# A linear-attention and SwiGLU block on one core: smaller first pieces, a split last block, and a scheduler that may wait

## The chip, the cores and the metric

The kernel runs on one core of a Trainium2 chip. The metric is the device time of one execution in microseconds (us). A profile's "span" is about 1.7 us shorter than that time. The profile of a kernel is one execution; the quoted times of the kernels before and after are of others.

## The reference

Layernorm of `x` (2048 x 1024), then two branches on the normalised `xn`: linear attention with 32 heads of 32, and a gated MLP with 3584 hidden columns. The output is `x + s * silu(mlp)`.

```python
def reference(A_x, A_wqkv, A_wo, B_x, B_w_gate, B_w_up, B_w_down):
    # ... qkv = xn @ wqkv; pq, pk = phi(q), phi(k); kv = pk^T v; s = (pq kv / pq z) @ wo
    # ... mlp = (silu(xn @ w_gate) * (xn @ w_up)) @ w_down
    x = A_x
    xn = _layernorm(x, axis=-1)
    s = _A_ref(xn, A_wqkv, A_wo)
    g = _silu(_B_ref(xn, B_w_gate, B_w_up, B_w_down))
    return x + s * g
```

## The kernel before

The matrix products are done with seven block products instead of eight (names `R00`, `T1` and so on). The sums and differences of blocks that this needs ("combinations") are VectorE's work, and PSUM results are joined by VectorE adds and ScalarE copies. The program runs in this order: a start (four x tiles: load, LN, transpose on TensorE, first k and v projections); the rest of k and v; then two passes over halves of the tokens, each with q, gate and up blocks, an `s` block (the attention output) and the down blocks.

Nothing is ordered by hand. Each operation is recorded with its reads and writes; a list scheduler that knows modelled durations fixes the order on every engine, and each engine then runs its list strictly in order. So a changed cost or position anywhere can reorder operations elsewhere.

```python
    def schedule(self):
        # ... dl: latest start for the modelled TensorE time; ready: when the inputs are there
            for e in self.ENGS:
                # ... TensorE has its own rule
                else:
                    rdy = [o for o in a if o.ready <= t]
                    o = min(rdy, key=lambda o: (o.dl - o.boost, o.idx)) if rdy else min(a, key=lambda o: (o.ready, o.dl))
```

```python
        def combos(v):          # four subtractions of whole 128x2048 blocks
            tt([v["R11"][1], v["R01"][1]], [v["T3"][1]], v["T3"][0], v["R11"][0], v["R01"][0], ALU.subtract, True)
            # ... T1, T2, T4

        # loads at the start, in this order
        for n, (fn, args) in enumerate(((x_load, (0,)), (x_load, (1,)), (wkv_load, (0, 1, 0)), (wkv_load, (0, 1, 1)),
                                        (wkv_load, (0, 0, 0)), (wkv_load, (0, 0, 1)), (x_load, (2,)), # ...

        # the normalisation of pq in pass p, hung on steps of the gate and up blocks
                if (k, n) == ("u", 1):
                    at = {"2_1": [partial(recip, p)]}
                if n == 2:
                    at = {w: [partial(normalise_part, p, "gu".index(k), h)] for h, w in enumerate(("2_1", "7_1"))}
                if (k, n) == ("g", 3):
                    at = {"2_1": [partial(combos, QV)], "7_1": [partial(x_inner, QV, qin, QIN_AT)]}
```

At the very end the last down product (step `4_1`) ends, ScalarE takes its silu, VectorE multiplies by `s`, TensorE transposes, VectorE adds `x`, and a store writes the result.

## Time and profile before

The time was 727.04 us in three runs (726.39 to 727.07).

| part of the profile | value |
|---|---|
| TensorE (PE) busy | 707.0 us, 97% of the span |
| VectorE (DVE) busy | 633.8 us, 87% |
| ScalarE (ACT) busy | 402.7 us, 56% |
| span | 725.4 us |

These lines are from the page of the kernel before: its span, the busy times, and the chain that ended last by engine.

```profile
span 725.4 us, 11190 instructions
PE 707.0 (97%) x4096; PEld 387.4 (53%) x4110; DVE 633.8 (87%) x1501; ACT 402.7 (56%) x773; POOL 14.2 (2%) x35
PE 87%; DVE 8%; DMA 2%; ACT 1%; issue 1%; SPq 0%; DVEq 0%
```

TensorE is the bound. Only its waits, the time before its first work and the time after its last are to be won. The Trainium skill (Trainium Kernel Development and Optimization, Performance Expectations) calls matmul busy time a bad metric for how close a kernel is to its roofline, because matmuls are pipelined. A 128x512 matmul is recorded as 0.379 us long but the next one starts 0.216 us later, so a wait of 0.16 us can hide inside "busy". I therefore also measured waits as the start of one matmul less the start of the one before, less the pace.

This is the table of waits, for TensorE alone, of the kernel before: waiting line, releaser, us in total, times, longest.

```profile
PE ps L233 <- DVE ps L376: 3.6, 6, 1.0
PE ps L233 <- ACT ps L365: 1.8, 2, 0.9
PE ps L233 <- ACT X L365: 1.6, 2, 1.2
...
PE ps L233 <- DMA H<-in_A_wqkv_dram: 0.4, 1, 0.4
```

Next come rows of the timeline of the kernel before, at its start: start in us, length, engine, line and operation; in brackets the idle time before it and what ended it.

```profile
3.58 0.69 DVE L680 BATCH_NORM_STATS2 stats<-W 128x6 f32<-128x512 bf16 x1 [2.39 <-DMA W<-in_A_x_dram]
...
6.43 0.55 DVE L694 TENSOR_SCALAR W<-W,mv,rstd 128x1024 f16<-128x1024 bf16 x1
...
8.12 2.76 PE L233 MATMUL ps<-H,X 128*128 128x512 bf16 x12 [0.47 <-ACT X L365]
8.25 1.23 DVE L376 TENSOR_TENSOR H<-H 128x2048 f16<-128x2048 bf16 x1 [0.97 <-DMA H<-in_A_wqkv_dram]
...
9.39 0.54 DVE L694 TENSOR_SCALAR W<-W,mv,rstd 128x1024 f16<-128x1024 bf16 x1
...
13.91 5.35 PE L233 MATMUL ps<-H,X 128*128 128x512 bf16 x23 [1.16 <-ACT X L365]
```

The LN of tile 1 (9.39) stands behind a 1.23 us combination, and TensorE later waits for that tile (13.91). The next rows, also of the timeline before, are those ahead of the `s` block of pass 1. Pass 2 repeats them near 534 us.

```profile
230.46 3.19 ACT L365 ACTIVATE H<-H,zc 128x512 bf16<-128x512 bf16 x5
...
234.47 0.64 ACT L365 ACTIVATE ps<-ps 128x512 f32<-128x512 f32 x1
...
235.16 1.90 PE L233 MATMUL ps<-X,W 128*128 128x512 f16 x8 [0.90 <-ACT ps L365]
...
235.74 1.22 DVE L376 TENSOR_TENSOR H<-H 128x2048 f16<-128x2048 f16 x1
...
236.87 0.69 DVE L376 TENSOR_TENSOR ps<-ps,TM 128x512 f32<-128x512 f32 x1
...
237.62 1.04 PE L233 MATMUL ps<-X,W 128*128 128x512 f16 x4 [0.56 <-DVE ps L376]
```

ScalarE works off five scale operations of the normalisation (3.19 us), and the copy that TensorE needs comes at 234.47. A whole combination on VectorE at 235.74 likewise delays the add at 236.87; the next wait ends at 237.62. The tail of the kernel before, in the same view:

```profile
718.31 0.60 ACT L365 ACTIVATE TM<-ps 128x512 f16<-128x512 f32 x1 [2.42 <-PE ps L233]
718.93 0.43 DVE L376 TENSOR_TENSOR TM<-TM 128x512 f16<-128x512 f16 x1 [2.26 <-ACT TM L365]
...
719.42 0.40 PE L240 MATMUL ps<-ident,TM 128*128 128x128 f16 x4 [1.15 <-DVE TM L376]
719.85 0.42 DVE L376 TENSOR_TENSOR TM<-ps,TM 128x512 bf16<-128x512 f16 x1 [0.49 <-PE ps L240]
```

### The profile page before, as it was taken

To read this page: it belongs to the slowest core of one execution; us is meant where nothing else is said; L and a number is where in the kernel's file an instruction comes from. 1 tells how busy PE (TensorE), PEld (TensorE's weight loads), DVE (VectorE), ACT (ScalarE), POOL (GpSimd) and SP (SyncE) were. 2 spreads that over 40 slices of the span, in tenths; PEclk is the share of its full clock that TensorE was granted. 3 is DMA by queue.
4 is the path that set the end of the run, shared out by engine and by line. 5 is a ranking of instruction groups with operands and counts; after the bars stand their busy time and mean duration, and the time that the engine had idled before them with its cause. 6 is when DMAs were issued, how large, how long until landed. Compare 5 with 4: busy or idle time off the path is not lost.

```text
span 725.4 us, 11190 instructions
## 1 busy us (share of the span) xinstructions
PE 707.0 (97%) x4096; PEld 387.4 (53%) x4110; DVE 633.8 (87%) x1501; ACT 402.7 (56%) x773; POOL 14.2 (2%) x35
## 2 busy tenths in 40 slices
PE   7999999999999999999999999999999999999996
PEld 3544445555555555556555454555555555565642
DVE  6999968989999998988966999999999989797852
ACT  3777554887659666654212156766786656531211
POOL 3101000000000000000000000000000000000000
PEclk9999999999999999999999999999999999999998
DMA  9345235145456343326595954231915241747563
GB/s 306 100 88 106 41 116 174 59 135 200 147 159 166 100 139 123 105 67 177 141 187 161 270 149 140 59 117 61 234 59 175 87 145 61 196 114 180 129 150 94
DMA packets 139127, 98.25 MB, mean 135 GB/s; under 512 B 33344, under 2 KB 136000, under 8 KB 139072
## 3 DMA queue, kind: packets, MB, share of 16 engines
q1 hardware_dynamic: 139072, 97.54, 47.9%
q8 instruction: 32, 0.52, 0.3%
q14 instruction: 23, 0.19, 0.1%
HBM read 77.59 MB, written 12.71 MB: 124 GB/s over the span
## 4 chain that ended last, share of the span: by engine, by line
PE 87%; DVE 8%; DMA 2%; ACT 1%; issue 1%; SPq 0%; DVEq 0%
PE ps L233 87%; DVE W L376 2%; DVE H L376 2%; DVE X L376 1%; DMA P<-x_scratch 1%; DMA H<-in_A_wqkv_dram 1%; DVE ps L376 1%; DVE TM L376 1%; SPq L379 0%; DVE P L376 0%; ACT TM L365 0%; ACT H L365 0%; PE ps L240 0%; ACT L365 0%; ACT ps L365 0%
## 5 line engine op out<-in xcount | busy, mean ns | idle before, releaser
L233 PE MATMUL ps<-X,W 128*128 128x512 f16 (+1 forms) x1344 | 289.9, 354 | 3.2 <-DVE ps L376 2.3
L365 ACT ACTIVATE TM<-ps 128x512 f16<-128x512 f32 (+2 forms) x353 | 186.1, 549 | 105.2 <-PE ps L233 103.1
L233 PE MATMUL ps<-H,W 128*128 128x512 f16 (+2 forms) x1090 | 218.4, 351 | 0.7 <-DVE ps L376 0.4
L376 DVE TENSOR_TENSOR W<-W 128x1024 f16<-128x1024 bf16 (+5 forms) x416 | 184.9, 479 | 5.5 <-PE ps L233 4.9
L233 PEld LDWEIGHTS ps<-X,W 128*128 128x128 f16 (+1 forms) x1344 | 130.4, 98 | 108.6 <-DVE ps L376 4.6
L233 PEld LDWEIGHTS ps<-H,W 128*128 128x128 f16 (+1 forms) x1096 | 106.6, 98 | 95.6 <-DVE ps L376 1.4
L365 ACT ACTIVATE ps<-ps 128x512 f32<-128x512 f32 (+1 forms) x172 | 84.7, 492 | 104.8 <-PE ps L233 101.3
L376 DVE TENSOR_TENSOR ps<-ps,TM 128x256 f32<-128x256 f32 (+1 forms) x250 | 130.7, 525 | 13.8 <-PE ps L233 12.5
L233 PE MATMUL ps<-P,W 128*128 128x256 f16 (+1 forms) x516 | 99.8, 319 | 1.2 <-ACT ps L365 0.9
L365 ACT ACTIVATE H<-ps 128x512 f16<-128x512 f32 (+1 forms) x126 | 75.0, 604 | 45.6 <-PE ps L233 45.5
L376 DVE TENSOR_TENSOR H<-H 128x1024 f16<-128x1024 f16 (+6 forms) x110 | 68.9, 640 | 1.1 <-DMA H<-in_A_wqkv_dram 1.0
L365 ACT ACTIVATE TM<-TM 128x512 f16<-128x512 f32 (+1 forms) x61 | 38.0, 629 | 52.6 <-DVE TM L376 52.6
L233 PEld LDWEIGHTS ps<-P,W 128*128 128x128 f16 (+1 forms) x516 | 50.0, 98 | 31.3 <-ACT ps L365 1.6
L233 PE MATMUL ps<-W 128*128 128x256 f16 (+1 forms) x330 | 62.1, 282 | 1.1 <-DVE ps L376 1.0
L376 DVE TENSOR_TENSOR H<-H,TM 128x512 f16<-128x512 f16 x112 | 45.1, 416 | 15.1 <-ACT H L365 14.9
L376 DVE TENSOR_TENSOR TM<-ps,TM 128x512 f32<-128x512 f32 (+1 forms) x60 | 40.7, 678 | 15.6 <-PE ps L233 15.1
L233 PEld LDWEIGHTS ps<-W 128*128 128x128 f16 (+1 forms) x330 | 31.5, 98 | 33.8 <-DVE ps L376 1.9
L233 PE MATMUL ps<-H,X 128*128 128x512 bf16 (+1 forms) x147 | 35.2, 379 | 2.2 <-ACT X L365 1.6
L233 PE MATMUL ps<-H,P 128*128 128x512 bf16 (+1 forms) x108 | 26.4, 379 | 0.1
L376 DVE TENSOR_TENSOR H<-ps,TM 128x512 f16<-128x512 f32 (+1 forms) x35 | 23.8, 680 | 2.2 <-PE ps L233 2.0
L233 PEld LDWEIGHTS ps<-H,X 128*128 128x128 f16 (+1 forms) x150 | 14.2, 98 | 18.5 <-ACT X L365 2.0
L376 DVE TENSOR_TENSOR TM<-TM,W 128x512 f16<-128x512 f16 (+1 forms) x39 | 14.1, 362 | 11.5 <-ACT TM L365 11.4
(95 smaller groups left out, 426.6 us busy)
## 6 DMA issues: line engine op xcount, KB each, us to landing
W<-in_B_w_gate_dram SPq DMA_DIRECT2D x14, 1024.0 KB, 5.3
W<-in_B_w_up_dram SPq DMA_DIRECT2D x13, 1024.0 KB, 5.6
W<-in_B_w_down_dram SPq DMA_DIRECT2D x14, 896.0 KB, 6.3
W<-in_A_x_dram SPq DMA_DIRECT2D x16, 256.0 KB, 3.0
H<-in_A_wqkv_dram SPq DMA_DIRECT2D x8, 512.0 KB, 8.0
H<-r_scratch SPq DMA_DIRECT2D x32, 128.0 KB, 3.8
W<-m_scratch SPq DMA_DIRECT2D x4, 1024.0 KB, 6.0
s_scratch<-TM SPq DMA_DIRECT2D x32, 128.0 KB, 2.6
```

The source lines that it names most:

```text
L233: last = h.matmul(o, l, r, start=st, stop=sp, skip_group_check=True)
L365: q = PL.op("act", reads, writes, lambda h: h.activation(o, i, func, **kw), nel(o) / (1000.0 if "bias" in kw or not isinstance(kw.get("sca ...
L376: return dve(reads, writes, lambda h: h.tensor_tensor(o, a, b, op), nel(o), 1.92 if fast else 0.96)
```

## The change

There are four parts. **Start:** x0 comes in two half loads on two queues; the first weight block is loaded ahead of x1; LN, transposes and first products work on smaller pieces. **Middle:** the normalisation and the combinations of the query blocks are issued earlier; combinations are cut in halves. **Tail:** the last down block finishes in two token halves, so the silu, the product, the transpose and the store after it are half as large. **Scheduler:** an engine other than TensorE and SP may leave a ready operation undone when a much more urgent one will be ready before it would end ("holding").

```diff
-TABLE, DMA_SLACK = 1.28, 2.0
+TABLE, DMA_SLACK, HOLD, YIELD = 1.28, 2.0, 0.1, 10
@@ schedule
-                    o = min(rdy, key=lambda o: (o.dl - o.boost, o.idx)) if rdy else min(a, key=lambda o: (o.ready, o.dl))
+                    soon = [o for o in a if o.ready > t]
+                    while rdy:
+                        o = min(rdy, key=lambda o: (o.dl - o.boost, o.idx))
+                        q = [q for q in soon if q.ready + HOLD < t + o.busy and q.dl + YIELD < o.dl] if e != "sp" else ()
+                        if not q:
+                            break
+                        rdy.remove(o)
+                    if not rdy:
+                        o = min(soon or a, key=lambda o: (o.ready, o.dl))
@@ combos: the four subtractions, each in two halves
+            for o, a, b in (("T3", "R11", "R01"), ("T1", "R01", "R00"), ("T2", "R11", "T1"), ("T4", "R10", "T2")):
+                for h in range(2):
+                    # ... half h of each
@@ x_load
+            for h, e in enumerate(("sp", "act")):
+                u = s.sub(h * KB, KB)
+                o, q = u.ap(), xf[0:128, h * 512:h * 512 + 512]
+                PL.op(e, [], [u.r], lambda h, o=o, q=q: h.dma_start(o, q), 0.47, sem=dsem("x%d" % (4 * h)), nbytes=128 * KB)
@@ loads
-        ... (x_load, (0,)), (x_load, (1,)), (wkv_load, (0, 1, 0)), (wkv_load, (0, 1, 1)),
+        ... (x_load, (0,)), (wkv_load, (0, 1, 0)), (x_load, (1,)), (wkv_load, (0, 1, 1)),
@@ places of the normalisation
-                    at = {"2_1": [partial(recip, p)]}
-                if n == 2:
-                    at = {w: [partial(normalise_part, p, "gu".index(k), h)] for h, w in enumerate(("2_1", "7_1"))}
+                    at = {"j1d": [partial(recip, p)]}
+                if (k, n) == ("g", 2):
+                    at = {"j1a": [partial(normalise_part, p, 0, 0)], "2_1": [partial(normalise_part, p, 0, 1)]}
+                if (k, n) == ("u", 2):
+                    at = {"j1a": [...], "2_1": [...], "4_1": [partial(combos, QV)]}
                 if (k, n) == ("g", 3):
-                    at = {"2_1": [partial(combos, QV)], "7_1": [partial(x_inner, QV, qin, QIN_AT)]}
+                    at = {"2_1": [partial(x_inner, QV, qin, QIN_AT)]}
@@ Down.finish, in place of the last 4_1 (cut)
+                for h, b in enumerate((self.sets[1].b, self.b2)):
+                    # ... the 14 products of 256 tokens each, then
+                    act([bank_r[b]], [gh.r], gh.ap(FP16), ps[b][:, 0:256], ACT.Silu)
+                    tt([gh.r, sh.r], [gh.r], gh.ap(FP16), gh.ap(FP16), sh.ap(FP16), ALU.mult, True)
+                    turns.append(h)
+                turn(1)
```

Also changed, and cut here: transposes of tile 0 in four pieces and of tile 1 in two, LN of both in two, the first projection piece in groups of two products, the wait of tile 1's statistics for tile 0's variance, and the modelled duration of four small GpSimd memsets.

More of the change, by code (lines that the diff above doesn't have):

```diff
@@ L478, in combos @@
         def combos(v):
-            tt([v["R11"][1], v["R01"][1]], [v["T3"][1]], v["T3"][0], v["R11"][0], v["R01"][0], ALU.subtract, True)
-            tt([v["R01"][1], v["R00"][1]], [v["T1"][1]], v["T1"][0], v["R01"][0], v["R00"][0], ALU.subtract, True)
-            tt([v["R11"][1], v["T1"][1]], [v["T2"][1]], v["T2"][0], v["R11"][0], v["T1"][0], ALU.subtract, True)
-            tt([v["R10"][1], v["T2"][1]], [v["T4"][1]], v["T4"][0], v["R10"][0], v["T2"][0], ALU.subtract, True)
+            for o, a, b in (("T3", "R11", "R01"), ("T1", "R01", "R00"), ("T2", "R11", "T1"), ("T4", "R10", "T2")):
+                for h in range(2):
+                    w = {}
+                    for nm in (o, a, b):
+                        ap, r = v[nm]
+                        n = len(r.keys) // 2
+                        w[nm] = ap[:, 2 * h:2 * h + 2, :], Region(r.keys[n * h:n * h + n])
+                    tt([w[a][1], w[b][1]], [w[o][1]], w[o][0], w[a][0], w[b][0], ALU.subtract, True)
         wz = TM.at(0, 1 * KB, FP16)
@@ L664, in x_load @@
             xslot[i] = s
-            dma([], [s.r], s.ap(), xf[i * 128:(i + 1) * 128, :], dsem("x%d" % s.k), 256 * KB).urgent = 10.0
+            if i:
+                dma([], [s.r], s.ap(), xf[i * 128:(i + 1) * 128, :], dsem("x%d" % s.k), 256 * KB).urgent = 10.0
+                return
+            for h, e in enumerate(("sp", "act")):
+                u = s.sub(h * KB, KB)
+                o, q = u.ap(), xf[0:128, h * 512:h * 512 + 512]
+                PL.op(e, [], [u.r], lambda h, o=o, q=q: h.dma_start(o, q), 0.47, sem=dsem("x%d" % (4 * h)),
+                      nbytes=128 * KB)
         def wkv_load(w, j, k):
@@ L679, in ln_tile @@
             sA, sB, mvr, ver, rsr, nmr = (named(n, j) for n in ("sA", "sB", "mv", "ve", "rs", "nm"))
-            o0 = dve([s.r], [sA], lambda h: h.bn_stats(stats[:, j, 0, :], xa[:, 0:512]), 512)
+            oA = dve([s.sub(0, KB).r], [sA], lambda h: h.bn_stats(stats[:, j, 0, :], xa[:, 0:512]), 512)
+            oB = dve([s.sub(KB, KB).r], [sB], lambda h: h.bn_stats(stats[:, j, 1, :], xa[:, 512:1024]), 512)
             if i == 1:
-                o0.preds.add(first_var[0])
-                first_var[0].succs.append(o0)
-            dve([s.r], [sB], lambda h: h.bn_stats(stats[:, j, 1, :], xa[:, 512:1024]), 512)
+                for o in (oA, oB):
+                    o.preds.add(first_var[0])
+                    first_var[0].succs.append(o)
             dve([sA, sB], [mvr], lambda h: h.bn_aggr(mv[:, j, :], stats[:, j, :, :]), 60)
@@ L693, in ln_tile @@
             if i < 2:
-                dve([s.r, mvr, rsr], [o.r], lambda h: h.tensor_scalar(
-                    oa, xa, mv[:, j, 0:1], rstd[:, j, :], ALU.subtract, ALU.mult), 1024, 2.6)
+                n = 512
+                for c in range(0, 1024, n):
+                    dve([s.r, mvr, rsr], [o.sub(2 * c, 2 * n).r], lambda h, c=c: h.tensor_scalar(
+                        oa[:, c:c + n], xa[:, c:c + n], mv[:, j, 0:1], rstd[:, j, :], ALU.subtract, ALU.mult), n, 2.6)
             else:
@@ L716, in t_tile @@
                 tb.extend((balloc_part(), balloc_part()))
-            for q, halves in enumerate(((0, 4), (4, 4)) if i == 0 else ((0, 8),)):
-                k0, n = halves
-                b = tb[(i + q) % 2]
+            n = (2, 4, 8, 8)[i]
+            for q, k0 in enumerate(range(0, KT, n)):
+                b = (tb + kvb)[q] if i == 0 else tb[(i + q) % 2]
                 pb = ps[b][:, 0:n * 64].bitcast(FP16).rearrange("p (k t) -> p k t", t=128)
-                pe_tr([s.r, ident_r], [bank_r[b]],
+                pe_tr([s.sub(k0 * 256, n * 256).r, ident_r], [bank_r[b]],
                       [(pb[:, k, :], xa[:, (k0 + k) * 128:(k0 + k + 1) * 128], ident[:, :]) for k in range(n)])
                 xr = xt_r(i, k0, n)
-                if q == 0 or i == 0:
+                if q % 2 == 0 or i == 0:
                     act([bank_r[b]], [xr], dst[:, k0:k0 + n], pb, ACT.Identity)
@@ L767, in build_kernel @@
         for q in range(4):
-            pool([], [named("vx1", q), vx_r[q], pool_chain], lambda h, q=q: h.memset(vext[q][:, :, 128:129], 1.0))
+            pool([], [named("vx1", q), vx_r[q], pool_chain], lambda h, q=q: h.memset(vext[q][:, :, 128:129], 1.0), 0.13)
         def k_evac(i, j, ap, r, kind):
@@ L784, in p_piece @@
             b = balloc(True)
-            for k in range(2):
-                ap, r = KVV[w]["R%d%d" % (k, j)]
-                pe_mm([xt_r(i, 4 * k, 4), r], [bank_r[b]],
-                      [(ps[b][:, :], xt_ap(i, 4 * k + q), ap[:, q, :], k + q == 0, k + q == 4) for q in range(4)])
+            n = 2 if (i, w, j) == (0, 0, 1) else 4
+            for k0 in range(0, KT, n):
+                ap, r = KVV[w]["R%d%d" % (k0 // 4, j)]
+                pe_mm([xt_r(i, k0, n), r], [bank_r[b]],
+                      [(ps[b][:, :], xt_ap(i, k), ap[:, k % 4, :], k == 0, k == KT - 1) for k in range(k0, k0 + n)])
             if w == 0:
@@ L842, in kv_set @@
             return st
-        for n, (fn, args) in enumerate(((x_load, (0,)), (x_load, (1,)), (wkv_load, (0, 1, 0)), (wkv_load, (0, 1, 1)),
+        for n, (fn, args) in enumerate(((x_load, (0,)), (wkv_load, (0, 1, 0)), (x_load, (1,)), (wkv_load, (0, 1, 1)),
                                         (wkv_load, (0, 0, 0)), (wkv_load, (0, 0, 1)), (x_load, (2,)),
@@ L1392, in do @@
                     tick()
+                elif t == "4_1" and (self.p, self.h) == (1, 1):
+                    self.finish()
                 elif t[0] == "4":
@@ L1401, in do @@
                         self.s3(w)
+                    if t == "7_1" and (self.p, self.h) == (1, 1):
+                        b = self.sets[1].b
+                        self.b2 = balloc()
+                        act([bank_r[b]], [bank_r[self.b2], bank_r[b]], ps[self.b2][:, 0:256], ps[b][:, 256:512], ACT.Identity)
                     tick()
@@ L1404, in do, with finish, turn @@
                     fn()
+            def finish(self):
+                p, c, (i, j) = 1, 3, (1, 0)
+                wv, wr = self.S[1][4]
+                sf = sf_rings[self.link].take()
+                dma([named("s", p, c, i)], [sf.r], sf.ap(FP16), s_scr[p, c, i, :, j * 512:j * 512 + 512],
+                    dsem("sf%s%d" % (sf.a.name, sf.off // KB)), 128 * KB)
+                g = fin_rings[self.link].take()
+                q, seen = self.xo[1, j]
+                xv = q.ap().rearrange("p (m n) -> p m n", n=256)
+                turns = []
+                def turn(h):
+                    gh = g.sub(h * KB // 2, KB // 2)
+                    b = balloc_part()
+                    pb = ps[b][:, 0:128].bitcast(FP16).rearrange("p (m n) -> p m n", n=128)
+                    pe_tr([gh.r, ident_r], [bank_r[b]], [(pb[:, m, :], gh.ap(FP16)[:, m * 128:(m + 1) * 128],
+                                                          ident[:, :]) for m in range(2)])
+                    v = xv[:, 2 * h:2 * h + 2, :]
+                    vr = q.sub(h * KB, KB).r
+                    tt([bank_r[b], vr], [vr], v[:, :, 128:256], pb, v[:, :, 128:256], ALU.add)
+                    row = p * 1024 + h * 256
+                    dma([vr], [], of[row:row + 256, c * 256:(c + 1) * 256].rearrange("(m p) n -> p m n", p=128), v,
+                        dsem("oz%d" % h), 128 * KB)
+                for h, b in enumerate((self.sets[1].b, self.b2)):
+                    for n in range(0, NPAIR, 2):
+                        tv, tr = self.t4[n // 2]
+                        pe_mm([wr, tr], [bank_r[b]], [(ps[b][:, 0:256], wv[:, n + k, :],
+                                                       tv[:, k, 256 * h:256 * h + 256], False, n + k == NPAIR - 1)
+                                                      for k in range(2)])
+                        if turns and n == 2:
+                            self.turn0()
+                        if turns and n == 8:
+                            turn(turns.pop())
+                    gh, sh = g.sub(h * KB // 2, KB // 2), sf.sub(h * KB // 2, KB // 2)
+                    act([bank_r[b]], [gh.r], gh.ap(FP16), ps[b][:, 0:256], ACT.Silu)
+                    tt([gh.r, sh.r], [gh.r], gh.ap(FP16), gh.ap(FP16), sh.ap(FP16), ALU.mult, True)
+                    turns.append(h)
+                turn(1)
             def keep(self, w):
@@ L1414, in fin @@
                 p, c = self.p, 2 * self.h + w
-                last = (p, c) == (1, 3)
                 sf = sf_rings[self.link].take()
@@ L1445, in turn @@
                 def turn():
-                    if not tbank:
-                        tbank.append(balloc_part())
-                    b = tbank[0]
+                    b = balloc_part()
                     pb = ps[b][:, 0:256].bitcast(FP16).rearrange("p (m n) -> p m n", n=128)
                     pe_tr([g.r, ident_r], [bank_r[b]], [(pb[:, m, :], g.ap(FP16)[:, m * 128:(m + 1) * 128], ident[:, :])
-                                                           for m in range(4)])
+                                                        for m in range(4)])
                     tt([bank_r[b], q.r], [q.r], xv[:, :, i * 128:i * 128 + 128], pb[:, :, :],
@@ L1454, in turn @@
                     done()
-                if last and (i, j) == (1, 0):
-                    defer(2, turn)
+                if (p, self.h, w, i, j) == (1, 1, 0, 1, 0):
+                    self.turn0 = turn
                 else:
@@ L1497, in down @@
             last_pair[0] = nxt
-        tbank = []
         combos(XV[0])
@@ L1553, in build_kernel @@
                 if (k, n) == ("u", 1):
-                    at = {"2_1": [partial(recip, p)]}
-                if n == 2:
-                    at = {w: [partial(normalise_part, p, "gu".index(k), h)] for h, w in enumerate(("2_1", "7_1"))}
+                    at = {"j1d": [partial(recip, p)]}
+                if (k, n) == ("g", 2):
+                    at = {"j1a": [partial(normalise_part, p, 0, 0)], "2_1": [partial(normalise_part, p, 0, 1)]}
+                if (k, n) == ("u", 2):
+                    at = {"j1a": [partial(normalise_part, p, 1, 0)], "2_1": [partial(normalise_part, p, 1, 1)], "4_1": [partial(combos, QV)]}
                 if (k, n) == ("g", 3):
-                    at = {"2_1": [partial(combos, QV)], "7_1": [partial(x_inner, QV, qin, QIN_AT)]}
+                    at = {"2_1": [partial(x_inner, QV, qin, QIN_AT)]}
                 if last_pair[0] is not None and (p, k, n) == (1, "q", 0):
```

## The prediction

> **What bounds the kernel.** TensorE. On the page it is busy 97% of 725.4 us and is 87% of the chain that ended last. Back to back, a 128x512 matmul follows the one before it every 0.216 us (84 in 18.3 us, timeline at 694). No matmul is removed (the last block's are cut into 256-column ones at about 0.109 us each), so the change can only take PE stalls, the time before PE starts and the time after it ends. Stalls, from start-to-start times against that pace:
>
> - Start: first real work at 7.03 us, then waits of 0.62 (ACT evacuation of x), 0.55 (a weight DMA landing at 11.22) and 1.31 us (transposed x1, at 13.91): 2.5.
> - Middle: 1.15 at 136 us (ACT, table load 1.28 ahead of it), 1.78 at 235 and 1.78 at 534 (ACT holding put1 behind five scale ops of the normalisation, 3.2 us; then a 1.22 us DVE combination ahead of a PSUM add), 1.11 at 416, 1.95 at 439 to 443 and 0.54 at 656 (urgent PSUM adds behind long DVE ops): 8.3.
> - Tail: last down matmul ends 718.3; ACT 0.60, DVE 0.43, transposes 0.40, DVE 0.42, then the store issued at 720.72 lands at 723.51; span ends 725.4: 7.1.
>
> Everything removable is about 12 us, so 2% (14.5 us) is out of reach.
>
> **Start.** The Trainium skill (Trainium Kernel Development and Optimization, Key Constraints) says DMAs from SP and ACT share the same 16 engines and only issue time is saved; the trace agrees: 6 to 17 us already moves about 360 GB/s. So two halves of x0 bring bn_stats forward by about 0.2 us at most. Reordering x1's statistics frees 0.6 us of DVE before x0's aggregate, and quarter transposes start PE work earlier: first projection matmul near 6.8 instead of 8.12. But the k-projection weights land at 6.8, 8.2, 9.7, 11.2 as before, so the first tile is still DMA-paced to about 12.1. The gain is x1: its LN (9.39) no longer waits behind a whole 1.23 us combination and its transposes fill the DMA wait, so the 1.31 stall goes. I take -1.8, some of it at risk because DVE is 96 to 99% busy from 20 to 80 us.
>
> **Middle.** Earlier normalisation, halved combinations and holding should remove the 235 and 534 stalls mostly (-2.6) and parts of 416, 439 and 656 (-1.8); but schedules come from a model, holding idles a DVE that is 98 to 100% busy at 220-280, 340-360 and 400-480, and new small stalls will appear (+0.4). Net -4.0.
>
> **Tail.** Half-size ACT (0.38, as the 128x256 ones), DVE mul 0.28, two transposes 0.29, DVE 0.28, 128 KB store about 2.4: saves about 1.5 of 5.2; the other transposes now run on PE before the end (+0.4). Net -1.1.
>
> Sum -6.9: **720.1 us**, 80% range **716.5 to 723.5**. Chances: faster by over 2% 0.01, within 2% 0.98, slower 0.01.
>
> **What would show it.** First projection matmul below 7.2 us; no wait over 0.6 near 13.9; the ACT and DVE waits at 235 and 534 under 0.7 in total each; PE's waits on "DVE ps" from 3.6 to about 2; PE busy nearly unchanged (707); last matmul to end of span 7.1 to about 5.7.
>
> **What would make it wrong.** Holding that shifts DVE work into saturated stretches and creates new PE stalls (then slower than 723); an earlier start given back at 26 us, where the first combined set waits for DVE's sums; or holding that clears nearly all middle stalls (then near 716).

## More of the kernel before

The two passes meet at the "turn" near 400 us, where the second half of the tokens is read back from DRAM.

## The result, and the profile after

The kernel after took 720.93 us (720.43 to 721.97, 4 runs) against 726.71 us (726.15 to 727.07, 4 runs): a ratio of 0.9923, 95% interval 0.9906 to 0.9940. Ratios are the mean time of one kernel's runs over that of the other's of the same rounds, so they are not quite the ratios of the medians. The gain is 5.8 us by medians, 0.8%.

The page of the kernel after, the same three lines:

```profile
span 721.6 us, 11255 instructions
PE 708.5 (98%) x4114; PEld 389.1 (54%) x4128; DVE 641.7 (89%) x1530; ACT 404.1 (56%) x777; POOL 13.8 (2%) x35
PE 82%; DVE 14%; DMA 1%; ACT 1%; issue 1%; SPq 0%; DVEq 0%
```

The span of this profiled execution is 721.6 us, but the timed ones had spans of 718.7 to 720.2 us. So the profiled one is not typical, and its start shows why. TensorE's waits, after:

```profile
PE ps L241 <- DMA H<-in_A_wqkv_dram: 1.9, 2, 1.6
PE ps L241 <- DVE ps L384: 1.8, 3, 0.8
```

The waits for "ACT ps" and "ACT X" are gone and those for "DVE ps" are halved, but waiting for weights went from 0.4 to 1.9 us. Here is the timeline after, at the start:

```profile
6.04 0.74 DVE L716 TENSOR_SCALAR W<-W,mv,rstd 128x512 f16<-128x512 bf16 x2 [0.68 <-POOL rstd L709]
...
7.28 1.04 PE L241 MATMUL ps<-H,X 128*128 128x512 bf16 x4
...
8.14 0.69 DVE L699 BATCH_NORM_STATS2 stats<-W 128x6 f32<-128x512 bf16 x1 [1.36 <-DMA W<-in_A_x_dram]
...
9.88 1.02 PE L241 MATMUL ps<-H,X 128*128 128x512 bf16 x4 [1.57 <-DMA H<-in_A_wqkv_dram]
...
11.29 1.89 PE L241 MATMUL ps<-H,X 128*128 128x512 bf16 x4 [0.38 <-DMA H<-in_A_wqkv_dram]
```

The first projection starts at 7.28 instead of 8.12, but x1 lands only at 8.12 and the next weights at 9.75. By the semaphore records, the 16 parts of the x1 load arrived between 5.38 and 8.12: 14 of them were there by 5.96, the last two came at 7.96 and 8.12, and the later loads show the same lag. The row at 11.29 has four matmuls in 1.89 us, about half the normal pace. The view by windows shows the granted clock there (stretch, its length, busy time of PE, PEld, DVE, ACT and POOL, granted clock, DMA share, GB/s):

```profile
11.22:14.64 3.42, 3.35 (x14) 1.75 (x15) 1.62 (x6) 0.92 (x2) 0.00 (x0) 0.50 1.09 356
```

Such halving is described by the Trainium skill (TensorE: Matmul & The Clock Gate, What's actually happening) as the default clock state that activity releases. Here it follows waits of 1.73 and 0.54 us (by the pace), though the four matmuls between the two still ran at full pace. The 14 matmuls from 11.29 to 14.66 hold 1.74 us of work and took 3.37 us: the slow clock cost 1.63 us, on top of the waits.

Ahead of the `s` block, the timeline after:

```profile
232.39 1.37 ACT L373 ACTIVATE H<-H,zc 128x512 bf16<-128x512 bf16 x2
...
233.14 2.11 PE L241 MATMUL ps<-X,W 128*128 128x256 f16 x10
...
233.61 0.64 ACT L373 ACTIVATE ps<-ps 128x512 f32<-128x512 f32 x1
...
235.31 1.03 PE L241 MATMUL ps<-X,W 128*128 128x512 f16 x4
```

Two scale operations are left here instead of five in a row, the copy comes in time, and TensorE has no wait (no bracket). The tail after:

```profile
716.04 0.38 ACT L373 ACTIVATE TM<-ps 128x256 f16<-128x256 f32 x1 [1.48 <-PE ps L241]
...
716.46 0.29 DVE L384 TENSOR_TENSOR TM<-TM 128x256 f16<-128x256 f16 x1 [0.23 <-ACT TM L373]
...
716.81 0.29 PE L248 MATMUL ps<-ident,TM 128*128 128x128 f16 x2 [0.80 <-DVE TM L384]
717.13 0.29 DVE L384 TENSOR_TENSOR TM<-ps,TM 128x256 bf16<-128x256 f16 x1 [0.38 <-PE ps L248]
```

Every step of the tail is shorter, as predicted (0.60 to 0.38, 0.43 to 0.29, 0.40 to 0.29, 0.42 to 0.29). From the last product's end (the start of its silu) to the end of the span it was 7.1 us and is 5.6 us.

**Where the time went, stage by stage.** TensorE runs its list in order, so progress can be compared: for a given amount of useful work (the sum of the paces of all matmuls after the warm-up ones: 0.2158 us for 512 columns, 0.109 for 256, 0.056 for 128 or 129, and 0.027 for each of 64 small ones that use 32 columns of the array), take the time at which that much is done, and subtract the work. The result, "lag", is the time lost so far. This table is worked out from the recorded starts of the weight loads, one per matmul, of which none is missing. All kernels in it are named below.

```
 work     before     after   a_again a_nohold2    b_hold   a_place      a_pw   n_start    a_tail
    6       9.36     10.53      7.82      7.82      9.97      7.79      7.57      9.42      7.47
   20       9.41     10.55      7.84      7.84     10.00      7.82      7.92      9.45      7.49
   30       9.43     11.54      8.83      8.83     10.02      8.81      8.98     10.51      8.48
  120       9.82     11.83      9.12      9.23     10.31      9.10      9.26     11.48      8.77
  210      11.24     13.31     10.59     10.65     11.78     10.57     10.74     12.91     10.25
  240      13.24     13.64     10.92     10.84     13.67     11.72     12.63     13.11     10.58
  255      13.24     14.10     11.38     10.88     13.68     11.86     12.64     13.15     11.04
  390      13.86     14.59     11.86     11.37     15.93     12.33     13.13     13.64     11.52
  450      17.28     16.14     14.80     12.84     17.76     14.13     14.61     15.14     14.08
  510      17.44     16.38     15.03     13.00     17.96     14.34     14.82     15.31     14.31
  540      19.44     17.16     15.82     13.23     19.85     15.79     16.71     15.54     15.10
  690      20.29     17.65     16.30     14.05     20.35     16.27     17.21     16.37     15.58
```

In the profiled execution after, the start lost 2.1 us (11.54 against 9.43 at 30) and the middle won 4.75 us (from +2.11 to -2.64 at 690). What follows 690 won 1.2 us: span less lag is 705.1 before and 703.9 after.

### The profile page after: what moved, and what is told of

Read it like the earlier page. It is cut to its first block, busy times and chain, and to the rows that moved or that the text cites. A ratio compares the mean times of both kernels' runs of the same rounds, so it can differ in the third digit from the quotient of the medians.

```text
span 721.6 us, 11255 instructions
## 1 busy us (share of the span) xinstructions
PE 708.5 (98%) x4114; PEld 389.1 (54%) x4128; DVE 641.7 (89%) x1530; ACT 404.1 (56%) x777; POOL 13.8 (2%) x35
## 4 chain that ended last, share of the span: by engine, by line
PE 82%; DVE 14%; DMA 1%; ACT 1%; issue 1%; SPq 0%; DVEq 0%
PE ps L241 82%; DVE H L384 5%; DVE ps L384 3%; DVE W L384 3%; DVE TM L384 1%; DMA H<-in_A_wqkv_dram 1%; DVE H L777 1%; ACT TM L373 0%; DVE P L384 0%; PE ps L248 0%; DVE X L384 0%; DVE H L955 0%; DVE TM L776 0%; SPq L387 0%; ACT L373 0%
## 5 line engine op out<-in xcount | busy, mean ns | idle before, releaser
L241 PEld LDWEIGHTS ps<-X,W 128*128 128x128 f16 (+1 forms) x1358 | 132.1, 98 | 104.4 <-DVE ps L384 1.5
L384 DVE TENSOR_TENSOR H<-H 128x1024 f16<-128x1024 f16 (+5 forms) x126 | 71.5, 580 | 0.6 <-ACT H L373 0.4
L384 DVE TENSOR_TENSOR TM<-ps,TM 128x512 f32<-128x512 f32 (+2 forms) x62 | 41.5, 669 | 13.4 <-PE ps L241 12.5
```

What stands on the lines that cost most here:

```text
L241: last = h.matmul(o, l, r, start=st, stop=sp, skip_group_check=True)
L384: return dve(reads, writes, lambda h: h.tensor_tensor(o, a, b, op), nel(o), 1.92 if fast else 0.96)
```

## The experiments

There are twelve runs; the table above shows seven of them (a_again is the kernel after, run once more). Lines that begin with `a_` change the kernel after, `b_` the kernel before, `n_` the kernel after without holding. Where runs come from different calls, I compare their ratios to the kernel before, since the kernel before itself moved from 726.5 to 727.2 us between calls. The last call (a_pw and the three `n_` runs) was also on another chip, and neither the kernel after nor a_nohold ran beside it. So the sizes of those four rest on the ratios; by the raw medians each of them would cost 0.3 to 0.9 us more.

### Tail back (a_tail)

```diff
-                elif t == "4_1" and (self.p, self.h) == (1, 1):
-                    self.finish()
-                    # ... and after step 7_1 the copy of half of the PSUM bank
-                if (p, self.h, w, i, j) == (1, 1, 0, 1, 0):
-                    self.turn0 = turn
+                if (p, c) == (1, 3) and (i, j) == (1, 0):
+                    defer(2, turn)
```

> The changed kernel with the old tail (last down block in one piece, last turn deferred). Theory: the new tail is worth 1.1 us (last weight load to end of span 5.86 us before, 4.78 after), so about 722.0 and a last stretch near 5.9 us. Rival: the tail only moved work onto TensorE, then no slower than 721. The first 30 us are the same program as the changed kernel's, so this is also a second look at its start: if the late landings of the profiled run of after (x1 at 8.12 us, first to last of its 16 parts 2.7 us apart) were chance, x1 lands near 6.5 here; if they belong to the new order of loads or to the second queue, they come again.

Measured: 722.59 us (722.52 to 722.76), ratio 0.9945 (0.9930 to 0.9959). So the new tail is worth about 1.7 us by medians. By the traces it is 1.5 us: the span less the lag at 690 is 705.4 us here and 703.9 in the kernel after and in its repeat. The theory holds, though its 1.1 us was too small: the stretch after the last weight load is 6.2 us here, not 5.9.

Its start is the same program as after's. Here x1 landed at 6.65 us, its parts 1.2 us apart, and the lag at 30 is 8.48 instead of 11.54. The same loads in the same order on the same queues landed x1 1.5 us apart, so the late landing was chance, not the order of loads. About half of the difference in lag (1.63 us) is the slow clock shown above, which a_tail and a_again don't have after their warm-up.

### x0 in one load (a_x0one)

```diff
-            if i:
-                dma([], [s.r], s.ap(), xf[i * 128:(i + 1) * 128, :], dsem("x%d" % s.k), 256 * KB).urgent = 10.0
-                return
-            for h, e in enumerate(("sp", "act")):
-                # ... two halves, on two queues
+            dma([], [s.r], s.ap(), xf[i * 128:(i + 1) * 128, :], dsem("x%d" % s.k), 256 * KB).urgent = 10.0
```

> The changed kernel with x0 as one 256 KB load on SP's queue; no load on ACT's. Theory A (the ACT queue's load puts one DMA engine behind): x1 lands before 6.8 us, first projection piece runs without the 1.7 us wait, time 719 or less. Theory B (chance, or the order of the loads): no different from the changed kernel, 720 to 721.5; bn_stats of x0 begins at 3.6 us either way, so the two halves are worth under 0.2 us.

Measured: 722.08 us (721.21 to 724.5), ratio 0.9942 (0.9923 to 0.9962). By the ratios that is slower than the kernel after by some 1.4 us, which neither theory expected, but the intervals overlap and two of the four runs (721.21, 721.51) are as fast as the kernel after. Theory A falls: without any load on ACT's queue, x1 landed as late (7.91 us). This fits what the Trainium skill says of the queues (Trainium Kernel Development and Optimization, Key Constraints): both feed the same 16 engines. Theory B is in doubt on the time: the median is above its 721.5. The profiled execution is the slowest of the four, and its timeline shows another reason:

```profile
8.01 0.69 DVE L692 BATCH_NORM_STATS2 stats<-W 128x6 f32<-128x512 bf16 x1 [2.60 <-DMA W<-in_A_x_dram]
...
8.62 0.72 DVE L709 TENSOR_SCALAR W<-W,mv,rstd 128x512 f16<-128x512 bf16 x2
...
9.07 0.90 PE L248 MATMUL ps<-ident,W 128*128 128x128 f16 x8 [2.19 <-DVE W L709]
```

With x0 as one load, the scheduler puts tile 1's first statistics ahead of tile 0's LN in VectorE's list. VectorE then stands waiting for x1 while x0, whose own inputs were ready about 6 us, is held up; its LN runs at 8.62 instead of 6.04. The halves gained almost nothing in arrival (statistics of x0 begin at 3.69 here and at 3.65 in the kernel after). Their effect in this trace was an order that doesn't depend on x1's arrival. One trace shows this, and the same trace has a slow clock too (0.50 from 9.47 to 12.88 us), which cost about 1.7 us. How much either explains of the 1.4 us in the timed runs is open.

### Without holding (a_nohold), and again beside the kernel after (a_nohold2, a_again)

```diff
-                    soon = [o for o in a if o.ready > t]
-                    while rdy:
-                        # ... the holding rule
+                    o = min(rdy, key=lambda o: (o.dl - o.boost, o.idx)) if rdy else min(a, key=lambda o: (o.ready, o.dl))
```

> The changed kernel without the holding rule in the list scheduler. Theory (earlier normalisation and halved combinations took the waits at 235 and 534 us away, holding the smaller ones at 416, 439, 656): waits at the place of 235 and 534 stay under 0.7 us each, 1.2 to 2.5 us come back elsewhere: 722.5. Rival (holding took nearly all): over 724.5, with waits of 1.5 us or more at both places.

Measured: 719.85 us (719.45 to 720.15), ratio 0.9906 (0.9891 to 0.9921). The waits at 235 and 534 stayed away, as the theory said. But both the theory and the rival had it slower; it was faster than the kernel after. So the two were run with more rounds, the kernel after unchanged under the name a_again:

> The changed kernel without the holding rule, again, beside the changed kernel itself. Theory from the first look (held order has waits of 0.37 and 0.6 us near 252 and 549 us that the unheld order lacks, and wins back only 0.54 at 650): 1 us faster than the changed kernel of the same rounds, 719.9. Rival (the first difference was the luck of the start): within 0.3 us of it.

> The changed kernel once more, on the chip and in the rounds of the next ones. 721 again (720.4 to 721.6). Its trace is a further look at its start: with x1 landing before 7 us (chance theory) the useful work of TensorE is then about 1 us behind less than in the old kernel at 25 us, and a 0.96 us wait near 29 us gives that back.

Measured: a_nohold2 719.81 us (719.74 to 719.85), ratio 0.9909 (0.9895 to 0.9922); a_again 720.79 us (720.25 to 721.98), ratio 0.9925 (0.9913 to 0.9938). This is what the theory from the first look expected. Holding costs 1.0 us here. The start is the same in both traces (lag 8.83 at 30), so it is not the luck of the start. The timeline of a_again, near 252 us:

```profile
251.48 0.68 DVE L384 TENSOR_TENSOR TM<-ps,TM 128x512 f32<-128x512 f32 x1
...
252.08 0.42 DVE L384 TENSOR_TENSOR ps<-ps,TM 128x256 f32<-128x256 f32 x1
...
252.21 2.13 PE L241 MATMUL ps<-H,W 128*128 128x512 f16 x13 [0.21 <-DVE TM L384]
```

and that of a_nohold2 at the same place, where TensorE streams 33 matmuls without a wait:

```profile
248.66 5.61 PE L233 MATMUL ps<-H,W 128*128 128x512 f16 x33
...
250.98 0.68 DVE L376 TENSOR_TENSOR TM<-ps,TM 128x512 f32<-128x512 f32 x1
251.58 0.42 DVE L376 TENSOR_TENSOR ps<-ps,TM 128x256 f32<-128x256 f32 x1
```

The lag table says where holding loses: 0.46 against 0.04 from 240 to 255, 0.79 against 0.23 from 510 to 540, and 2.94 against 1.47 around the turn (390 to 450; 2.56 in a_tail, which starts as early and holds too). Of this last difference, a wait at 437 (0.72 us held, 0.36 unheld) comes back in every held trace. It wins 0.35 us at 650, where the unheld order waits 0.54 and the held one 0.19. These two profiled executions are 2.2 us apart, more than the medians, and the turn is the part that varies: the kernel after lost only 1.55 us there, and a_whole and a_pw, which hold too, 1.47 and 1.48. That holding lengthens the turn beyond the wait at 437 is not shown. The trace a_again also shows what happens to an earlier start. At the turn the kernel after waited only 0.61 us at 408, this run 1.78 us at 407. It came there 2.7 us earlier, but its first read-back load of the second half was complete at 395.69, after's at 396.00. In these two traces 1.4 of the 2.7 us are gone by 450. That the loads and VectorE set the pace of the turn is the likely reason; no run tests it.

The gain of a start can be seen without the chance of the profiled run. In a_again, the lag at 20 is 1.6 us smaller than before's; at 30 it is 0.6 us smaller, because of a new wait:

```profile
29.37 0.82 PE L241 MATMUL ps<-H,W 128*128 128x512 f16 x3 [0.79 <-DVE ps L384]
```

VectorE's add ends at about the same distance behind TensorE whatever the start was, because the add in turn waits for TensorE's product (VectorE was idle for 0.32 us before it, in a_again as in after): this wait was 0.96 us by the pace in a_again, a_tail, a_place and after alike, though they started up to 3 us apart.

### Holding alone (b_hold)

The old kernel with the rule added, no other line changed.

> The old kernel with the holding rule alone. Same theory: 725.2 (1.5 off 726.7), the waits at 235 and 534 us stay at 1 us or more each because ACT is full with the normalisation's scale operations there. Rival: 723 or less, both waits gone.

Measured: 725.55 us (725.01 to 727.17), ratio 0.9982 (0.9966 to 0.9999); before had 726.63. Its profile fell on an execution with the span of before (725.5). The two waits stay, as the theory said; its table of TensorE's waits has

```profile
PE ps L241 <- ACT ps L373: 1.8, 2, 0.9
```

exactly as before. So holding is worth about 1 us on the old order (the interval reaches from 0.1 to 2.5 us) and costs 1 us on the new one.

### The old places (a_place), whole combinations (a_whole), and both (a_pw)

```diff
 a_place: the block of `at = ...` assignments as in the kernel before
 a_whole:
-            for o, a, b in (("T3", "R11", "R01"), ...): for h in range(2): ...
+            tt([v["R11"][1], v["R01"][1]], [v["T3"][1]], v["T3"][0], v["R11"][0], v["R01"][0], ALU.subtract, True)
+            # ... T1, T2, T4 whole
 a_pw: both
```

> The changed kernel with the normalisation, the query combinations and the inner sums issued at their old places. Theory (ACT full with scale operations just ahead of the s block is what stopped TensorE at 235 and 534 us): about 2 us of wait come back at these two together, 723; waits put down to ACT. Rival (halved combinations did it): under 0.6 us comes back, 721.5.

> The changed kernel with the combinations in whole 128x2048 operations again. Theory: a fraction, 0.6 us at each of the two s blocks at most and less than 1 us at the start, where x1's LN waits behind a whole one: 721.5 to 722.3. Rival (halving did most): over 723.

> The changed kernel with both the old places and the whole combinations. Undone alone these cost 1.3 us and -0.3 us. Theory (each alone hides most of the waits ahead of the s blocks, so either undo finds the other still there): together they cost 3 us or more, about 724, with waits near 235 and 534 us of 1.7 us or more each. Rival (their effects add): about 1 us, 721.8, and waits of 1.1 us each.

Measured: a_place 722.09 us (721.58 to 723.2), ratio 0.9943 (0.9928 to 0.9959); a_whole 720.45 us (720.23 to 720.61), ratio 0.9917 (0.9904 to 0.9931); a_pw 723.0 us (722.81 to 724.3), ratio 0.9949 (0.9933 to 0.9966). The kernel after has 0.9925 and 0.9923.

The old places cost 1.3 us and bring ScalarE's wait back, as this timeline of a_place shows:

```profile
229.66 3.81 ACT L373 ACTIVATE H<-H,zc 128x512 bf16<-128x512 bf16 x6
...
233.33 0.62 ACT L373 ACTIVATE ps<-ps 128x512 f32<-128x512 f32 x1
...
234.01 2.86 PE L241 MATMUL ps<-X,W 128*128 128x512 f16 x11 [0.41 <-ACT ps L373]
```

Theory (about 2 us of wait, put down to ScalarE) against rival (under 0.6): by the pace the waits in a_place were 0.57 and 0.30 us here and 0.57 and 0.48 us in pass 2, against 1.78 us at each place before. With whole combinations as well (a_pw) they are 1.06 and 0.61 us at each place: the old waits, nearly whole. With whole combinations and the new places (a_whole) there is none. So the new places alone clear both waits (n_whole below shows the same without holding); halving alone halves them. For a_whole both expectations were wrong: it was not slower at all. Undone singly the two look like 1.3 us and nothing; undone together they cost 1.8 us by ratios and bring back 3.3 us of waits. Part of that is made up elsewhere: a_pw doesn't have the kernel after's waits at 252 and 549, and neither does a_place. My theory was right about the waits (1.67 us each, just under the 1.7 expected) and wrong about the time (724 expected).

### The old start (n_start), and x1 first (n_x1first)

n_start takes `x_load`, `ln_tile`, `t_tile`, `p_piece` and the order of loads from the kernel before. n_x1first changes one line:

```diff
-        ... (x_load, (0,)), (wkv_load, (0, 1, 0)), (x_load, (1,)), (wkv_load, (0, 1, 1)),
+        ... (x_load, (0,)), (x_load, (1,)), (wkv_load, (0, 1, 0)), (wkv_load, (0, 1, 1)),
```

> The changed kernel without holding (719.8) and with the old start: x0 in one load, x1 ahead of the weights, whole LN, old transposes. Theory: the new start wins 1.6 us of TensorE's time by 20 us and gives 0.96 back near 29 us, so undoing it costs 0.6 us: 720.4, the wait near 29 us gone, and TensorE behind its work by 9.4 to 10.0 us at 30 us instead of 8.8. Rival (the start is worth my predicted 1.8): 721.6.

> The changed kernel without holding, with x1 loaded ahead of the first weights as before, all else of the new start kept. Theory: no gain and no loss over 0.3 us (719.5 to 720.1): the first projection waits for the weights landing at 8.2, 9.7 and 11.2 us in either order. Rival (an x1 that lands 2 us later holds up the start): 0.5 us or more faster.

Measured: n_start 722.01 us (721.94 to 722.11), ratio 0.9930 (0.9915 to 0.9945), against 0.9906 and 0.9909 with the new start. So the new start is worth about 1.6 us in this order by the ratios (2.2 by the raw medians, which are of two chips), close to my predicted 1.8 and not the 0.6 of the theory. At 20 us the theory's 1.6 us is there (9.45 against 7.84). The wait near 29 us is gone, as expected. But two others have come, in the timeline of n_start:

```profile
36.70 1.04 PE L233 MATMUL ps<-H,X 128*128 128x512 bf16 x4 [0.87 <-DVE TM L759]
...
50.30 1.04 PE L233 MATMUL ps<-H,X 128*128 128x512 bf16 x4 [0.40 <-DVE TM L759]
```

VectorE is 96 to 99% busy from 20 to 80 us in the kernel before. That a fixed list on an engine that full turns small shifts into waits somewhere is my reading, not tested; the kernel before had the luck to have none there.

n_x1first took 721.32 us (721.17 to 721.67), ratio 0.9921 (0.9906 to 0.9936): about 1.0 us slower than with the weights first, against both the theory and the rival. It also puts both of x1's statistics ahead of x0's LN; its first transpose starts at 7.10 instead of 6.53 (a_nohold) or 6.72 (a_nohold2), and waits of 1.23 and 0.38 us come at 30.5 and 36.5, where a_nohold2 has one of 0.96 at 29.4. Its weights landed late in the profiled execution (7.67, 9.06, 10.57, 12.05), so which of these makes the 1.0 us is not settled.

### Whole combinations without holding (n_whole)

The edit of a_whole on a_nohold.

> The changed kernel without holding and with whole combinations. Theory: halving is worth nothing once normalisation is placed early, with or without holding: 719.5 to 720.1. Rival (halving needs no holding to pay): 720.8 or more.

Measured: 721.7 us (720.27 to 721.88), ratio 0.9921 (0.9907 to 0.9936), about 1.0 us slower than a_nohold by ratios. The rival is nearer: without holding, halving seems to pay. The waits at 235 and 534 are absent here too; what came back in the middle is after the turn, with 0.96, 0.52 and 0.47 us at 437, 438 and 441 us. These are the very waits of the kernel before at 439 to 443. In a_nohold2 there is one of 0.36 (and 0.9 us ahead of it at the turn, which n_whole lacks). With holding there is one of 0.72, with whole combinations (a_whole, b_hold) and with halves (after) alike. So at this place holding and halving replace each other, as places and halves do ahead of the `s` block. But that is not all: the trace is behind from the start. The last part of x1 landed at 8.10 us (6.02 in a_nohold, 6.76 in a_nohold2), and 1.0 to 1.3 us of the about 2 us by which n_whole is behind those two at 690 are there at 6 us of useful work. Whether the timed runs share this late start is not known, and one of the four was at 720.27. So the size of what halving pays without holding stays open.

## Why the prediction was right

The time was in the range (720.93 and, again, 720.79, against 720.1) and the gain 5.8 us against 6.9. The parts deserve a closer look, because two of them were right for partly wrong reasons.

- **The bound, right.** Everything removable was put at 12 us. The best version run here is at 719.8. PE busy time is nearly unchanged, as predicted: it rose from 707.0 to 708.5 us while the time fell.
- **Start, mis-sized and partly unseen.** Predicted -1.8. In typical traces it is -1.6 at 20 us of work and -0.6 at 30 us, after the 0.96 us wait near 29. I had named this ("given back at 26 us, where the first combined set waits for DVE's sums") as what could go wrong, and then not subtracted it. The wait was for a PSUM add on VectorE, not for the sums. "The 1.31 stall goes" held. "The first tile is still DMA-paced to about 12.1" held (weights land at 8.46, 9.96 and 11.46 in a_again). What I missed is that the landings themselves vary: the last part of x1 landed between 5.95 and 8.12 us in executions whose start is the same but for VectorE's operations. And the profiled run lost 1.63 us more to a slow clock, which the prediction has no term for. The 360 GB/s of the prediction, all issued from SP, showed that the engines were full, not that two queues share them; a_x0one bears on that.
- **Middle, right in size; one step wrong.** Predicted -4.0; the lag between 30 and 690 fell by 4.75 in the profiled run and by 3.4 in a_again and 3.8 in a_tail. The placement step held: the waits at 235 and 534 are gone, 3.56 us in all (predicted 2.6), and with the scale operations back on ScalarE part of the wait comes back. The new places move the normalisation, the query combinations and the inner sums together, and no run tells their shares apart. The three waits named at 416, 439 and 656 fell from 3.60 us to 1.52 in after, 2.69 in a_again and 2.54 in a_tail, so by 2.1, 0.9 and 1.1 (predicted 1.8). The step that failed is that holding helps there: without it they fell by 1.8 (a_nohold2), which is no less than the held average, and the 0.35 us that holding wins at 650 are lost again at 437. Holding also adds the waits at 252 and 549; on the new order its net is +1.0 us. I had the right fear ("holding idles a DVE that is 98 to 100% busy", +0.4) and gave it less than half its size.
- **Tail, right.** Predicted -1.1; 1.2 to 1.7 by the traces and the undo run. Each duration estimated from 128x256 operations elsewhere (0.38, 0.28, 0.29, 0.28) came out within 0.01 us.
- **Signs to look for.** "First projection matmul below 7.2": 7.28 in one trace and 7.99 in another; the warm-up matmuls at half clock, which stand ahead of it in the list, ran until about 7.1 us there. "PE's waits on DVE ps to about 2": 1.8 and 3.0. "No wait over 0.6 near 13.9", the waits at 235 and 534, PE's busy time and the last stretch (5.6 us): held.

The best version is the changed kernel without the holding rule: 719.85 and 719.81 us, 0.9% below the kernel before.

## What to carry to other kernels

When undoing one part of a change shows no loss, the part isn't proved idle: two parts can clear the same wait, so undo them together as well, and count waits at the place rather than only the total. A scheduling rule has to be measured on the order it will run with; here the same rule won 1 us on the old kernel and lost 1 us on the new. In a static, in-order list, an operation that waits for a load must not stand ahead of one on the critical path that has its data, because landings differ by microseconds from one execution to the next.

## What the Trainium skill lacked or had wrong

- DMA: Bandwidth & Descriptors gives a fixed cost and a rate per load (for loads issued from GpSimd; these were issued from SP). I found no figure in it for how far apart the 16 parts of one load arrive: for the same 256 KB load early in the program, the first and last part were 0.6 us apart in one execution (a_whole) and 2.7 us in another (after), and the lag stayed on the loads behind it.
- TensorE: Matmul & The Clock Gate (What you observe) puts the change to full clock around 4 us into sustained activity, within 0.5 us. It says further down that it varies with the run, and the traces agree with that more than with the half microsecond: at the same program start, weight loads 0.43 us apart, the mark of the slow clock, last appear at 4.38 us in after and at 6.51 us or later in a_tail. That is 3.0 and at least 5.1 us after the first matmul at 1.41.
- ScalarE: Activation LUTs (What ACT_TABLE_LOAD costs) gives 1.28 us for the load and 1.38 us of drain, 2.66 us in all. In the kernel before the load took 1.28 us as stated, but the operation ahead of it ended at 134.21 and the one behind it began at 135.52: 1.31 us in all, and no drain to be seen there. The six later loads of that trace show the same.
- Key Constraints of Trainium Kernel Development and Optimization (issuing from several engines saves only issue time) was borne out: the statistics of x0 began at 3.58 us with one load before, at 3.65 with two queues after and at 3.69 with one load in a_x0one.
